# A three-block kernel: where the folded weights' loads stand in the first phase's written order

## The chip, the cores and the metric

The kernel runs on one core of a Trainium2 chip. The metric is the time of one execution on the device in microseconds, as the median of several runs. One execution was also recorded by the hardware profiler; every row below is from that one.

## What is computed

Three blocks follow one another, for 4 batches of 576 tokens. Cut to what matters here:

```python
# 1: attention over a window of 128 keys, 8 heads of 64 -> x: 4 x 576 x 512
# 2: gated block
h = np.maximum(x @ w_in, 0.0)                     # 512 -> 1024
u, v = h[..., :512], h[..., 512:]
v_n = (v - mean(v)) / np.sqrt(var(v) + 1e-06)      # per token
v_s = einsum('ts,bsd->btd', w_spatial, v_n) + b_spatial
x = (u * v_s) @ w_out
# 3: four experts of attention (wq, wk, wv, wo), two of them chosen per token by x @ w_gate
```

Between block 2 and block 3 nothing stands but matrix products, so the kernel never forms the second block's output: it multiplies w_out by the third block's wq, wk, wv and w_gate once, and lets block 3 read G = u * v_s. That product is the fold, and its operands are the folded weights.

## The kernel before

**Two phases.** The first phase makes attention and the gated block for the four batches, one after another, and stores G in HBM. Then comes the fold (`fold`, line 937: 96 matmuls), and the second phase runs the experts.

**Split numbers.** Every float32 operand of a product is kept as two tiles, a rounded one (cast on ScalarE, `split`, line 265, or its like) and the remainder (a subtraction on VectorE, `lo_part`, line 261), and every product is three passes of matmuls over them (`PASSES`).

**The written order.** The first phase is a list of short names in three strings, OPENING, FIRST and SECOND. `step` (line 809) turns a name into instructions. Those that matter here, for batch b, tile of tokens t, half of the tokens s, and block of 128 columns m:

- `V.b.t.n`, `r`, `bn`, `ag`: v before its normalisation (12 matmuls of 128x512 in three passes), its eviction with the ReLU on ScalarE (line 723), its mean and variance on VectorE (lines 726 and 727).
- `n.b.t.ln`, `.ex`, `.r0` to `.r3`: one over the root of the variance, for tiles 0 to 2 at once (`normal_ops`, line 730; ScalarE lines 736 and 737, VectorE lines 738 to 741).
- `N.b.t.sc`, `.hi`, `.lo`: v scaled (VectorE line 745), rounded (ScalarE line 749), its remainder (VectorE line 263).
- `U.b.s.m.n`, `ur`: u (12 matmuls of 128x288, line 777) and its eviction with the ReLU (ScalarE line 780).
- `P.b.m.s.n`, `pm`, `gs`: v_s (line 792), the product with u on VectorE (line 800), the store of G by SP (line 877).

All of these products go through three PSUM banks (`psD`, line 247), so a product can only begin once the product three before it has been evicted.

**Who sets the order.** TensorE runs its matmuls as they are written, in the whole kernel. For ScalarE, VectorE, GpSimd and SP, a scheduler that simulates the program may reorder instructions, except where `written` holds (from line 242 to its closing): there they too run as written. OPENING stands within `written`; its last part is the end of batch 2 and the beginning of batch 3. FIRST and SECOND are the rest of batch 3, put in a queue (`Dense`) and pulled from between other steps.

**The folded weights' loads.** Behind OPENING, still within `written`, the program makes the loads of chunks 0 and 1 of wcat (wq, wk, wv and w_gate side by side, 128 rows of 772 each; `take_wcat`, line 900). Then `written` closes, and there follow the loads of chunks 2 and 3 and of w_out (`wt`, line 957), the four chunks' casts and remainders (`load_wcat`, line 932: lines 266 and 263), and the loads of batch 0's G (`load_g`, line 966: line 974), whose tail is cast into `both` (line 986). The program pulls FIRST in between:

```python
    for name in OPENING.split():
        step(name)
    ...
    for k in range(2):
        take_wcat(k)
    written.close()
    for name, names in (("u3_1", FIRST), ("s3", SECOND)):
        dense.add(rest(names), cost(names), name=name)
    ...
    for k in (2, 3):
        dense.pull(1000.0)
        later.popleft()()
    dense.through("u3_1")
```

All of these transfers are issued by SP, in one queue.

Of the kernel before, what the change touches and what calls it, by code (L numbers as in the profile page):

```python
# [103 lines left out]
    P2.0.0.2 pm2.3.1 gs2.3 a17 pm2.0.0 R18.1 pm2.0.1 gs2.0 xc17 P2.1.0.0 V3.3.0 xs17 xh17 R18.0 P2.2.0.0 P2.2.0.1 xl17 P2.1.0.1 P2.1.0.2 g18.1.0  # L104
    V3.3.1 g18.1.1 pm2.1.0 V3.3.2 g18.0.0 V3.1.0 r3.3 g18.0.1 bn3.3 V3.1.1 ag3.3 n3.3.ln V3.1.2 n3.3.ex n3.3.r0 n3.3.r1 P2.2.0.2 n3.3.r2 r3.1 n3.3.r3
    N3.3.sc a18 pm2.2.0 bn3.1 ag3.1 xc18 P2.2.1.0 P2.1.1.0 xs18 P2.2.1.1 xh18 P2.2.1.2 xl18 U3.1.0.0 pm2.2.1 P2.1.1.1 gs2.2 V3.2.0 N3.3.hi U3.1.0.1
    U3.1.0.2 V3.2.1 ur3.1.0 P2.1.1.2 V3.2.2
"""
FIRST = """
    pm2.1.1 N3.3.lo gs2.1 U3.1.3.0 r3.2 U3.1.3.1 bn3.2 U3.1.3.2 U3.1.2.0 ag3.2 n3.2.ln ur3.1.3 U3.0.2.0 n3.2.ex n3.2.r0 U3.1.2.1 n3.2.r1 n3.2.r2  # L110
    U3.1.2.2 n3.2.r3 N3.1.sc U3.0.2.1 N3.2.sc ur3.1.2 N3.1.hi U3.0.2.2 N3.0.sc N3.2.hi U3.0.3.0 N3.1.lo N3.0.hi U3.0.1.0 N3.2.lo ur3.0.2 U3.0.3.1
    N3.0.lo U3.0.3.2 P3.2.0.0 ur3.0.3 U3.0.1.1 P3.2.0.1 U3.0.1.2 P3.2.1.0 ur3.0.1 P3.2.0.2 P3.2.1.1 pm3.2.0 P3.1.0.0 P3.1.0.1 U3.1.1.0 P3.2.1.2
    P3.1.0.2 pm3.2.1 gs3.2 U3.1.1.1 pm3.1.0 U3.1.1.2 U3.0.0.0 ur3.1.1 P3.1.1.0 P3.0.0.0 U3.0.0.1 P3.0.0.1 U3.0.0.2
"""
SECOND = """
    P3.1.1.1 ur3.0.0 P3.1.1.2 P3.0.0.2 pm3.1.1 gs3.1 P3.0.1.0 pm3.0.0 P3.0.1.1 P3.0.1.2 P3.3.1.0 pm3.0.1 P3.3.1.1 gs3.0 P3.3.0.0 P3.3.0.1 P3.3.1.2
# [1255 lines left out]
```

## Time and profile before

| | us |
|---|---|
| median of 3 runs | 432.82 |
| the runs | 433.19, 429.93, 432.82 |
| the profiled execution | 429.61 |
| its span, first to last instruction | 427.9 |
| TensorE busy (matmuls) | 410.8 (96% of the span) |
| VectorE, ScalarE, GpSimd busy | 316.0, 242.7, 171.2 |

The span is the part of the execution that the rows cover; 1.7 us lie around it. Busy time is the time in which an engine works on an instruction, not that in which it waits for one. TensorE's granted clock is 1.00, its higher level (2.4 GHz), in all forty slices of the span.

### The profile page before, as it was taken

The page shows a single profiled execution, that of the slowest core. Times are in us where ns is not written, and L with a number is a line of the kernel's source. Part 1 is how long each engine was busy: PE and PEld are TensorE (multiplying, and loading weights), DVE is VectorE, ACT ScalarE, POOL GpSimd, SP SyncE. Part 2 cuts the span into 40 slices and gives each one's busy share as a digit, 9 for nine tenths or more (in the row PEclk, how much of TensorE's full clock was granted, in tenths as well). Part 3 has the DMA queues.
Part 4 walks back from the last instruction along what each step waited for, and adds up shares of the span by engine and source line. Part 5 has one row for each costly group of instructions (what it writes and reads, how often), then busy time and mean ns, then how long its engine had stood idle before and what let it go on. Part 6 is the DMA issues. An engine that isn't in the chain of part 4 may idle for free.

```text
span 427.9 us, 12099 instructions
## 1 busy us (share of the span) xinstructions
PE 410.8 (96%) x4399; PEld 367.5 (86%) x4399; DVE 316.0 (74%) x1061; ACT 242.7 (57%) x757; POOL 171.2 (40%) x265
## 2 busy tenths in 40 slices
PE   6789999999999999999996999999999999999996
PEld 5567798799899998899996999999999998988884
DVE  5998999999899968796445322649888788678541
ACT  6898768847465465463225202656666557556642
POOL 3575644537306644432300000139665653544100
PEclk9999999999999999999999999999999999999999
DMA  8997367858846865324294170211879978898884
GB/s 258 383 289 284 111 180 209 277 138 273 263 145 156 266 182 159 95 76 108 60 347 158 42 230 2 58 54 26 214 203 279 250 158 242 210 269 223 221 261 126
DMA packets 76943, 80.06 MB, mean 187 GB/s; under 512 B 18002, under 2 KB 52946, under 8 KB 76500
## 3 DMA queue, kind: packets, MB, share of 16 engines
q1 hardware_dynamic: 76740, 79.15, 63.2%
q8 instruction: 35, 0.57, 0.6%
q14 instruction: 24, 0.20, 0.1%
q10 hardware_dynamic: 144, 0.13, 0.1%
HBM read 49.64 MB, written 29.62 MB: 185 GB/s over the span
## 4 chain that ended last, share of the span: by engine, by line
PE 73%; DMA 8%; ACT 7%; DVE 6%; POOL 2%; issue 2%; SPq 2%; DVEq 0%; ACTq 0%; POOLq 0%
PE pq L1042 12%; PE pg L792 10%; PE pv L714 7%; PE pu L777 7%; PE pvB L1070 6%; PE pxB L1239 6%; PE pout_None L1257 6%; PE psB L1136 4%; PE pw L946 4%; ACT p L286 3%; DMA st_wc<-in_wcat 3%; DMA raw<-in_w_in 3%; DMA carry<-p 3%; PE px L679 3%; PE pg L795 2%
## 5 line engine op out<-in xcount | busy, mean ns | idle before, releaser
L286 ACT ACTIVATE p<-p,st 128x128 f32<-128x128 f32 x144 | 56.5, 396 | 23.3 <-DVE st L285 13.4
L792 PE MATMUL pg<-wsp,vn 128*128 128x288 f32 x384 | 59.9, 297 | 2.1 <-ACT vn L749 2.0
L777 PE MATMUL pu<-x,win 128*128 128x288 f32 x384 | 58.6, 298 | 2.0 <-ACT u L780 1.7
L777 PEld LDWEIGHTS pu<-x,win 128*128 128x128 f32 x384 | 53.5, 188 | 5.1 <-ACT u L780 2.2
L792 PEld LDWEIGHTS pg<-wsp,vn 128*128 128x128 f32 x384 | 54.1, 188 | 4.4 <-ACT vn L749 2.2
L714 PE MATMUL pv<-win,x 128*128 128x512 f32 x216 | 57.3, 398 | 0.3 <-ACT x L700 0.3
L565 POOL TENSOR_TENSOR p<-p,st 128x512 f32<-128x512 f32 (+1 forms) x28 | 32.4, 1161 | 61.5 <-DVE st L563 29.2
L1042 PE MATMUL pq<-x,W 128*128 128x288 f32 x384 | 56.8, 297 | 0.0
L1042 PEld LDWEIGHTS pq<-x,W 128*128 128x128 f32 x384 | 52.5, 188 | 1.6 <-issue 0.8
L1160 ACT ACTIVATE pB<-pB,stB 128x128 f32<-128x128 f32 (+4 forms) x72 | 41.7, 581 | 13.7 <-DVE stB L1152 7.5
L298 POOL TENSOR_SCALAR pB<-pB,stB 128x384 f32<-128x384 f32 (+4 forms) x64 | 35.9, 581 | 28.8 <-DVE stB L1169 13.8
L714 PEld LDWEIGHTS pv<-win,x 128*128 128x128 f32 x216 | 38.4, 188 | 8.3 <-issue 1.0
L1152 DVE CUSTOM_DVE_ANT_0 pB<-psB,trit 128x128 f32<-128x128 f32 (+3 forms) x64 | 27.9, 485 | 6.0 <-PE psB L1136 5.7
L285 DVE CUSTOM_DVE_ANT_0 p<-ps,relm 128x128 f32<-128x128 f32 x128 | 30.1, 281 | 3.0 <-DMA carry<-p 2.8
L1186 DVE STREAM_TRANSPOSE pB<-pB 128x1024 f32<-128x1024 f32 (+3 forms) x28 | 26.9, 980 | 1.7 <-POOL pB L298 1.7
L286 ACT ACTIVATION_READ_ACCUMULATOR p<-p,st 128x1 f32 x144 | 27.5, 191 | 0.0
L602 POOL TENSOR_SCALAR_AFFINE_SELECT pU<-pT 128x512 f32<-128x512 f32 (+1 forms) x26 | 18.7, 727 | 21.1 <-DMA pT<-carry 21.0
L1070 PE MATMUL pvB<-W,x 128*128 128x260 f32 x192 | 27.1, 284 | 0.0
L1239 PE MATMUL pxB<-pTB,vt 128*64 128x128 f32 (+2 forms) x480 | 26.4, 260 | 0.0
L1257 PE MATMUL pout_None<-wo,o 128*128 128x512 f32 x102 | 26.3, 401 | 0.0
L1239 PEld LDWEIGHTS pxB<-pTB,vt 128*64 128x64 f32 (+1 forms) x480 | 23.2, 136 | 2.8 <-issue 1.1
L1070 PEld LDWEIGHTS pvB<-W,x 128*128 128x128 f32 x192 | 24.7, 188 | 0.8 <-issue 0.7
(195 smaller groups left out, 932.9 us busy)
## 6 DMA issues: line engine op xcount, KB each, us to landing
carry<-p SPq DMA_DIRECT2D x96, 64.0 KB, 2.4
pT<-carry SPq DMA_DIRECT2D x24, 256.0 KB, 3.1
q<-in_qP SPq DMA_DIRECT2D x20, 256.0 KB, 3.5
g_dram<-g SPq DMA_DIRECT2D x16, 288.0 KB, 3.6
gf<-g_dram SPq DMA_DIRECT2D x16, 288.0 KB, 5.0
raw<-in_w_in SPq DMA_DIRECT2D x8, 512.0 KB, 6.6
v<-in_v SPq DMA_DIRECT2D x16, 256.0 KB, 4.3
mid<-pB SPq DMA_DIRECT2D x16, 256.0 KB, 4.9
```

The costliest lines, as they stand in the source:

```text
L285: lambda: nc.vector.tensor_tensor_reduce(s_view, ps_view, tab, -0.125, FLT_MAX, ALU.add, ALU.min, nm),
L286: lambda: nc.scalar.activation(s_view, s_view, AF.Exp, bias=nm, scale=-1.0, accum_out=sm),
L298: nc.gpsimd.tensor_scalar(p, p, r, 0.0, op0=ALU.mult, op1=ALU.add)
L565: ops["m"] = lambda: nc.gpsimd.tensor_tensor(blocks, blocks, sm.unsqueeze(1).unsqueeze(3).to_broadcast([P, 4, n, 32]), op=ALU.mult)
L714: nc.tensor.matmul(pv, x[i][:, k, t0 : t0 + P], win[j][:, k, 512:1024], start=(n == 0 and k == 0), stop=(n == 2 and k == 3))
L777: nc.tensor.matmul(pu[:, :HALF], win[i][:, k, m * P : (m + 1) * P], x[j][:, k, c], start=(n == 0 and k == 0), stop=(n == 2 and k == 3))
L792: nc.tensor.matmul(pg[:, :HALF], vn[i][k][:, m * P : (m + 1) * P], wsp[j][:, k, c], start=(n == 0 and k == 0), stop=False)
L1042: nc.tensor.matmul(pq[:, :HALF], W[i][c0 // CUT][:, k, c0 % CUT : c0 % CUT + P], G[j][:, k, c], start=(n == k == 0), stop=(n == 2 and k == 3))
L1070: nc.tensor.matmul(pv[:, :260], rows, W[j][1][:, k, 512 - CUT :], start=(n == k == 0), stop=(n == 2 and k == 3))
L1160: nc.scalar.activation(part(i), part(i), AF.Exp, bias=st[:, i : i + 1], scale=-1.0, accum_out=st[:, 4 + i : 5 + i])
L1239: nc.tensor.matmul(px[64 * o : 64 * o + 64, pr, :qn], vt[:kb, c, (2 * pr + o) * 64 : (2 * pr + o) * 64 + 64], rhs(pr, c, o), start=(c == 0 ...
L1257: nc.tensor.matmul(po[:, : c.stop - c.start], o2[i][:, pr, :], wos[j][:, pr, c], start=(n == pr == 0), stop=(n == 2 and pr == 1))
```

## The change

36 names go from FIRST to the end of OPENING, in the same sequence: from the last product of batch 2 (`pm2.1.1`) through v's normalisation of batch 3 and its last remainder (`N3.0.lo`). The rest of the program's text stays as it is. So for these steps the four engines beside TensorE run in the order of the names, and the two loads that stand behind OPENING (chunks 0 and 1 of wcat) come after them.

```diff
@@ OPENING, its end
-    U3.1.0.2 V3.2.1 ur3.1.0 P2.1.1.2 V3.2.2
+    U3.1.0.2 V3.2.1 ur3.1.0 P2.1.1.2 V3.2.2 pm2.1.1 N3.3.lo gs2.1 U3.1.3.0 r3.2 U3.1.3.1 bn3.2 U3.1.3.2 U3.1.2.0 ag3.2 n3.2.ln ur3.1.3 U3.0.2.0
...
+    N3.0.hi U3.0.1.0 N3.2.lo ur3.0.2 U3.0.3.1 N3.0.lo
@@ FIRST, its beginning
-    pm2.1.1 N3.3.lo gs2.1 U3.1.3.0 r3.2 U3.1.3.1 bn3.2 U3.1.3.2 U3.1.2.0 ag3.2 n3.2.ln ur3.1.3 U3.0.2.0 n3.2.ex n3.2.r0 U3.1.2.1 n3.2.r1 n3.2.r2
...
+    U3.0.3.2 P3.2.0.0 ur3.0.3 U3.0.1.1 P3.2.0.1 U3.0.1.2 P3.2.1.0 ur3.0.1 P3.2.0.2 P3.2.1.1 pm3.2.0 P3.1.0.0 P3.1.0.1 U3.1.1.0 P3.2.1.2 P3.1.0.2
```

ScalarE, from the eviction of v's tile 2 of batch 3 on, before. A name ends in a number of the build; `wc00` and `wc01` are the rounded chunks 0 and 1, `vr3_2` is v of batch 3, tile 2, `vn0_1` its rounded tile 1, `u3` is u's column block 3, and `both0_0` is the tail of batch 0's G.

```order
L723 ACTIVATE vr3_2_3606<-pv3_2_3516 128x512
L266 CAST wc00_3578<-st_wc0_3545 128x772
L780 ACTIVATE u3_109<-pu3_3_1_3601 128x288
L736 ACTIVATE vs3_3176<-vs3_3176,eps_147 128x3
L266 CAST wc01_3579<-st_wc1_3547 128x772
L737 ACTIVATE vs3_3176<-vs3_3176 128x3
L780 ACTIVATE u2_108<-pu3_2_1_3619 128x288
L780 ACTIVATE u2_108<-pu3_2_0_3627 128x288
L749 CAST vn0_1_111<-vr3_1_3438 128x512
L749 CAST vn0_2_112<-vr3_2_3606 128x512
L780 ACTIVATE u3_109<-pu3_3_0_3661 128x288
L749 CAST vn0_0_110<-vr3_0_3224 128x512
```

The same place now, as far as the next eviction of u:

```order
L736 ACTIVATE vs3_3176<-vs3_3176,eps_147 128x3
L780 ACTIVATE u3_109<-pu3_3_1_3548 128x288
L737 ACTIVATE vs3_3176<-vs3_3176 128x3
L780 ACTIVATE u2_108<-pu3_2_1_3564 128x288
L749 CAST vn0_1_111<-vr3_1_3438 128x512
L749 CAST vn0_2_112<-vr3_2_3553 128x512
L749 CAST vn0_0_110<-vr3_0_3224 128x512
L780 ACTIVATE u2_108<-pu3_2_0_3572 128x288
L986 CAST both0_0_3799<-gf0_3786 128x4x64
L780 ACTIVATE u3_109<-pu3_3_0_3604 128x288
L266 CAST wc00_3656<-st_wc0_3623 128x772
L266 CAST wc01_3657<-st_wc1_3625 128x772
```

The two casts moved from ahead of v's normalisation to behind it; behind them now stands the eviction of u's block 1. The cast of G's tail stood behind v's last rounding and ahead of that eviction, and now stands ahead of the second eviction of block 3. On VectorE the two remainders moved in the same way, from ahead of line 738 to ahead of the first product of batch 3 (line 800).

SP, from the first store of G in this stretch on, before (`g2_2` is G of batch 2, block 2; `gf0` is batch 0's G on its way back):

```order
L877 DMA g_dram_84<-g2_2_3476 128x576
L902 DMA st_wc0_3545<-in_wcat 128x772
L902 DMA st_wc1_3547<-in_wcat 128x772
L957 DMA wt1_3577<-wt_dram_83 128x512 x2
L974 DMA gf0_3786<-g_dram_84 128x576 x4
L877 DMA g_dram_84<-g2_1_3401 128x576
```

And now:

```order
L877 DMA g_dram_84<-g2_2_3476 128x576
L957 DMA wt1_3655<-wt_dram_83 128x512 x2
L974 DMA gf0_3786<-g_dram_84 128x576 x4
L877 DMA g_dram_84<-g2_1_3401 128x576
L902 DMA st_wc0_3623<-in_wcat 128x772
L902 DMA st_wc1_3625<-in_wcat 128x772
```

The two loads moved behind the last two pieces of w_out, the four loads of G and one store.

## Rows read from the trace of the kernel before

**Rows 1.** Waits of TensorE, whole run: us in total, times, longest.

```profile
PE pg L792 <- ACT vn L749: 2.0, 1, 2.0
PE pu L777 <- ACT u L780: 1.7, 2, 1.2
```

**Rows 2.** Busy time by stage: PE, PEld, DVE, ACT, POOL, clock, DMA, GB/s.

```profile
220.00:225.00 5.00, 4.64 (x35) 4.41 (x34) 0.88 (x2) 0.83 (x2) 0.00 (x0) 1.00 1.03 398
224.00:232.00 8.00, 4.25 (x28) 3.56 (x28) 5.76 (x12) 5.02 (x12) 0.64 (x1) 1.00 0.64 243
232.00:253.00 21.00, 20.93 (x153) 20.70 (x152) 6.22 (x12) 3.60 (x8) 0.43 (x3) 1.00 0.34 113
253.00:300.00 47.00, 47.00 (x344) 45.35 (x343) 25.25 (x75) 22.12 (x61) 15.08 (x26) 1.00 0.15 43
```

**Rows 3.** Timeline of TensorE: start us, us, what, idle before and its releaser.

```profile
219.70 4.94 PE L777 MATMUL pu<-x,win 128*128 128x288 f32 x36
225.87 0.80 PE L777 MATMUL pu<-x,win 128*128 128x288 f32 x4 [1.22 <-ACT u L780]
227.18 1.84 PE L777 MATMUL pu<-x,win 128*128 128x288 f32 x12 [0.52 <-ACT u L780]
231.03 0.80 PE L792 MATMUL pg<-wsp,vn 128*128 128x288 f32 x4 [2.00 <-ACT vn L749]
...
233.24 1.22 PE L792 MATMUL pg<-wsp,vn 128*128 128x288 f32 x8
...
234.56 1.75 PE L792 MATMUL pg<-wsp,vn 128*128 128x288 f32 x12
236.15 0.70 PE L777 MATMUL pu<-x,win 128*128 128x288 f32 x4
...
250.57 2.61 PE L946 MATMUL pw<-wc,wt 128*128 128x384 f32 x14
```

**Rows 4.** Timeline of ScalarE.

```profile
219.90 0.60 ACT L723 ACTIVATE vr<-pv 128x512 f32<-128x512 f32 x1 [1.34 <-PE pv L714]
224.67 0.83 ACT L266 CAST wc<-st_wc 128x772 fp32r<-128x772 f32 x1 [4.17 <-DMA st_wc<-in_wcat]
225.41 0.40 ACT L780 ACTIVATE u<-pu 128x288 f32<-128x288 f32 x1
225.71 0.29 ACT L736 ACTIVATE vs<-vs,eps 128x3 f32<-128x3 f32 x1
...
229.02 1.14 ACT L749 CAST vn<-vr 128x512 fp32r<-128x512 f32 x2 [1.59 <-DVE vr L745]
```

**Rows 5.** Timeline of VectorE: tile 3's statistics and scaling, then tile 2's.

```profile
207.96 0.18 DVE L727 BATCH_NORM_AGGREGATE vs<-vs 128x2 f32<-128x6 f32 x1
...
209.51 0.55 DVE L745 TENSOR_SCALAR vr<-vr,vs 128x512 f32<-128x512 f32 x1
...
221.26 0.18 DVE L727 BATCH_NORM_AGGREGATE vs<-vs 128x2 f32<-128x6 f32 x1
225.54 0.96 DVE L263 TENSOR_TENSOR wc<-st_wc,wc 128x772 fp32r<-128x772 f32 x1 [4.09 <-ACT wc L266]
...
228.44 1.46 DVE L745 TENSOR_SCALAR vr<-vr,vs 128x512 f32<-128x512 f32 x3
```

**Rows 6.** Timeline of SP's issues: start us, us, what.

```profile
217.13 1.40 SPq L902 DMA_DIRECT2D st_wc<-in_wcat  x2
...
220.47 2.64 SPq L974 DMA_DIRECT2D gf<-g_dram  x4
224.71 20.46 SPq L877 DMA_DIRECT2D g_dram<-g  x3
```

**Rows 7.** DMA, 215:231 (busy in 40 slices; issues, KB, us to landing), then 217.1:217.5.

```profile
DMA  9999887999999999999999999999999999410000
...
gf<-g_dram SPq DMA_DIRECT2D x4, 288.0 KB, 7.1
...
st_wc<-in_wcat SPq DMA_DIRECT2D x1, 386.0 KB, 7.5
```

More of the change, by code (lines that the diff above doesn't have):

```diff
@@ L106 @@
     N3.3.sc a18 pm2.2.0 bn3.1 ag3.1 xc18 P2.2.1.0 P2.1.1.0 xs18 P2.2.1.1 xh18 P2.2.1.2 xl18 U3.1.0.0 pm2.2.1 P2.1.1.1 gs2.2 V3.2.0 N3.3.hi U3.1.0.1
-    U3.1.0.2 V3.2.1 ur3.1.0 P2.1.1.2 V3.2.2
+    U3.1.0.2 V3.2.1 ur3.1.0 P2.1.1.2 V3.2.2 pm2.1.1 N3.3.lo gs2.1 U3.1.3.0 r3.2 U3.1.3.1 bn3.2 U3.1.3.2 U3.1.2.0 ag3.2 n3.2.ln ur3.1.3 U3.0.2.0
+    n3.2.ex n3.2.r0 U3.1.2.1 n3.2.r1 n3.2.r2 U3.1.2.2 n3.2.r3 N3.1.sc U3.0.2.1 N3.2.sc ur3.1.2 N3.1.hi U3.0.2.2 N3.0.sc N3.2.hi U3.0.3.0 N3.1.lo
+    N3.0.hi U3.0.1.0 N3.2.lo ur3.0.2 U3.0.3.1 N3.0.lo
 """
 FIRST = """
-    pm2.1.1 N3.3.lo gs2.1 U3.1.3.0 r3.2 U3.1.3.1 bn3.2 U3.1.3.2 U3.1.2.0 ag3.2 n3.2.ln ur3.1.3 U3.0.2.0 n3.2.ex n3.2.r0 U3.1.2.1 n3.2.r1 n3.2.r2
-    U3.1.2.2 n3.2.r3 N3.1.sc U3.0.2.1 N3.2.sc ur3.1.2 N3.1.hi U3.0.2.2 N3.0.sc N3.2.hi U3.0.3.0 N3.1.lo N3.0.hi U3.0.1.0 N3.2.lo ur3.0.2 U3.0.3.1
-    N3.0.lo U3.0.3.2 P3.2.0.0 ur3.0.3 U3.0.1.1 P3.2.0.1 U3.0.1.2 P3.2.1.0 ur3.0.1 P3.2.0.2 P3.2.1.1 pm3.2.0 P3.1.0.0 P3.1.0.1 U3.1.1.0 P3.2.1.2
-    P3.1.0.2 pm3.2.1 gs3.2 U3.1.1.1 pm3.1.0 U3.1.1.2 U3.0.0.0 ur3.1.1 P3.1.1.0 P3.0.0.0 U3.0.0.1 P3.0.0.1 U3.0.0.2
+    U3.0.3.2 P3.2.0.0 ur3.0.3 U3.0.1.1 P3.2.0.1 U3.0.1.2 P3.2.1.0 ur3.0.1 P3.2.0.2 P3.2.1.1 pm3.2.0 P3.1.0.0 P3.1.0.1 U3.1.1.0 P3.2.1.2 P3.1.0.2
+    pm3.2.1 gs3.2 U3.1.1.1 pm3.1.0 U3.1.1.2 U3.0.0.0 ur3.1.1 P3.1.1.0 P3.0.0.0 U3.0.0.1 P3.0.0.1 U3.0.0.2
 """
```

## The prediction

> **What bounds the kernel now.** I read the waits of TensorE first. In the whole run it waits little, and the two largest entries behind the first 40 us are neighbours: 2.0 us for the rounded tiles of v, once, and 1.7 us for u's evictions, twice [rows 1]. The busy time by stage says where. TensorE has 4.64 us of work in the 5 us from 220 to 225 and 4.25 in the 8 us from 224 to 232, and from 232 on it is full: 20.93 of 21 us, then 47.00 of 47 [rows 2]. So TensorE is the bound, and one hole, 224 to 232, belongs to the stretch that the change rewrites.
>
> Its size comes from the starts of the matmuls. A 128x288 matmul takes 0.1325 us when nothing is in its way: twelve lie between the starts at 234.56 and 236.15 [rows 3]. The 36 that begin at 219.70 would let the next start at 224.47; it starts at 225.87, 1.40 late. Four more (0.53) end at 226.40; the next start is at 227.18, 0.78 late. Twelve more (1.59) end at 228.77; the first gating matmul of batch 3 (pg3_2_0) starts at 231.03, 2.26 late. Together 4.43 us [rows 3], somewhat over the 3.7 us that the waits sum to, because a restart also refills the pipeline.
>
> Who makes the hole stands in the rows of ScalarE and VectorE. ScalarE takes v's last tile out at 219.90 and next has the cast of the folded weights' chunk 0, which starts at 224.67 after 4.17 us of waiting for its load [rows 4]. Behind it in the same queue stand the eviction of u that TensorE needs first (225.41), the logarithm of the normalisation, the second cast, and so on to the rounding of v's tiles from 229.02 [rows 4]. VectorE is in the same place: the statistics of tile 2 are aggregated at 221.26, and its next instruction is chunk 0's remainder at 225.54, 4.09 us of waiting for that cast; the three scalings follow at 228.44 [rows 5]. The load itself was issued at 217.13 and took 7.5 us, in a burst in which the loads of batch 0's G take 7.1 [rows 6, 7]; the engines that move data are full from 215 to about 229 us [rows 7], at 398 GB/s [rows 2].
>
> **The change part by part.** Nothing is computed more or less; TensorE's own order is the same instruction for instruction, and GpSimd's too. Two loads (386 KB each), two casts and two remainders move.
>
> Removed from the path: on ScalarE and VectorE the wait for chunk 0 and the four instructions between v's statistics and its normalisation. What is late next? The chain from aggregate to scaling stands undisturbed in the same trace for tile 3: 207.96 to 209.51, 1.55 us [rows 5]. From 221.26 that gives 222.81; one eviction of u stands between logarithm and exponential now, at most 0.3 us more, as its neighbours in ScalarE's queue start 0.30 apart (225.41 to 225.71) [rows 4]: 223.1. Three scalings take 1.46 [rows 5], so 224.6. The two casts of v at 229.02 take 1.14 together [rows 4]; three take 1.7, and they begin behind u's eviction that waits for TensorE's 28th matmul of the 36 (219.70 + 3.71 = 223.4, evicted near 224.0): last cast near 225.6. TensorE, running through, comes to pg3_2_0 at 219.70 + 52 x 0.1325 = 226.6. So v is ready 1 us before it is asked for, and each of the three starts that were late is covered: the whole 4.43 us is open to be won.
>
> Put in elsewhere, three things. First, the two loads are issued behind w_out's last pieces, G of batch 0 and one store of G. They cost issue time on SP only, but the landing matters. The load of chunk 0 now has the place in SP's queue that the last load of G had, which was issued about 222.8 (220.47 + 2.64, less its own issue) [rows 6]. The bytes of the burst are the same, and it ends about 229 us by the share of busy transfer engines [rows 7]; that last load of G took 7.1, landing at 229.9 [rows 6, 7]. I take the end of the burst, 229.0 to 229.9, as landing of the last folded load (chunk 1), middle 229.5.
>
> Second, on ScalarE the casts now stand ahead of the eviction of u's column block 1 (u1_107 out of pu3_1_0), and on VectorE the remainders stand ahead of the first gating product (g3_2). Counted from pg3_2_0, TensorE wants the bank of the former 4.06 us later (in before, 231.03 to 234.56 plus four matmuls) and that of the latter 5.12 us later (236.15) [rows 3], now 230.7 and 231.7. Cast of chunk 1 at 229.5 for 0.83 [rows 4], eviction of 0.4 behind it: free near 230.6. Remainder from 230.4 for 0.96, product of 0.45 behind it: near 231.7. Both arrive with nothing to spare: 0 to 0.5 us of new waiting; I take 0.2.
>
> Third, the cast of G's tail (both0_0) is now ahead of the eviction of u's block 3 (pu3_3_0), whose bank TensorE wants 2.21 us after pg3_2_0 (233.24) [rows 3], now 228.8. G's loads have two loads fewer ahead: 2 x 395 kB at 398 GB/s [rows 2] is 2.0 us, so the last lands near 227.9, the tail is cast by 228.3, the eviction is done near 228.6. Hidden, by 0.2 us; if that cover goes, it is the same sub-microsecond wait.
>
> The Trainium skill (DMA: Bandwidth & Descriptors, section "Where 436 GB/s comes from") says that for transfers between HBM and SBUF HBM's share of a core binds, about 358 GB/s; this trace shows 398 in that stretch [rows 2], so the lower rate does not bind here. By that page's rate the last 6.5 us before 229.5 would stretch to an estimated 7.2, and the sum would lose another 0.7 us.
>
> Sum: -4.43 + 0.2 = -4.2 us. Where does it go afterwards? Behind 232 us TensorE has no wait in the list [rows 1, 2], and the loads of batch 1's G wait for casts that wait for TensorE, so all of it moves forward together. The profiled execution takes 429.61 (span 427.9 and 1.7 around it) and would take 425.4. The runs shown are 429.93, 432.82 and 433.19, so the profiled one lies 3.2 under their median of 432.82, by nothing this trace explains. On the median the forecast is 432.82 - 4.2 = 428.6 us.
>
> Bounds. Upper end of the gain: 4.43, no new wait. Lower end of this case: chunk 1's load takes the 7.5 us that the folded load at 217.13 took [rows 7], from an issue at 222.8, and lands at 230.3; that is 0.7 of waiting, and with a restart of up to 0.3 the gain is 3.4. On the median 428.4 to 429.4.
>
> **The rivals.**
> Partly given back: a new wait takes the place of the old. Beyond 229.6 us each microsecond by which chunk 1 lands late is one of waiting. If SP issues the two loads only where it now issues the store ahead of them, 224.71 [rows 6], they land 7.5 us on, about 232.2; the new wait is 2.6 and the gain 1.8: 431.0 us. For it: SP stood 1.6 us before that store. Against: it stood there for the landing of chunk 0's load, which is no longer ahead of it.
>
> Given back downstream: the gain is real at 232 us but phase two is paced by transfers. 432.8 us, no change. Against: TensorE full from 253 to 300 with hardly any traffic, 43 GB/s [rows 2].
>
> Slower: both casts now block ScalarE's queue in front of evictions that TensorE needs, where before they blocked it one stage earlier. It decides from a landing of chunk 1 at 229.6 + 4.4 = 234.0. With two latencies of 7.5 us [rows 7] in a row, each load waiting for the one before, it would be 222.8 + 15 = 237.8: 3.8 us slower, 436.6. Against: two loads were in flight together in before, issued back to back at 217.13 [rows 6].
>
> That the change does not do what it says is half true: of four chunks only 0 and 1 move, chunks 2 and 3 stay ahead as before. TensorE has no wait for them: the two entries above are the largest behind the first 40 us, and both belong to the hole [rows 1, 3]. So that costs nothing.
>
> **How the numbers follow.** A measurement of this kernel tells about 1% (4.3 us) from no change. Main case 0.64; partly given back 0.19; no change 0.10; slower 0.07. The main case lies right at the 1% line, 4.2 against 4.33. The runs of before lie in two groups 3 us apart with the median in the upper, so a median in the lower group would read as clearly faster; I count 0.45 of the main case as faster, 0.19 as same. With 0.01 of the partial case: faster 0.46, same 0.47, slower 0.07. The range goes from the lower group's full gain, 425.2, down to 425.0, to the partial case and a little more, 431.5.
>
> **What would show it.** Right: no wait of TensorE over 0.5 us between 220 and 235; logarithm near 221.5; pg3_2_0 near 226.6; casts of chunks 0 and 1 near 228.5 and 229.5; first fold matmul near 246.4 in place of 250.57 [rows 3]. Wrong in the middle step: ScalarE's largest wait there is again for the folded load, now behind 229.6, with evictions of u or products of G late after it. Wrong at the end: fold 4 us earlier, span not.

## The result, and the profile after

| | before | after |
|---|---|---|
| median, 7 runs each, us | 432.82 | 427.33 |
| lowest and highest | 429.55 to 434.32 | 425.77 to 428.70 |
| the profiled execution | 429.61 | 428.70 |
| its span | 427.9 | 426.8 |

The ratio of after to before is 0.9891, with a 95% interval of 0.9852 to 0.993: faster by 1.1%.

The two profiled executions are only 0.9 us apart, so the gain can't be read from their spans. After's execution came to the stretch in question late: the 36 matmuls of u that [rows 3] begin with start at 222.13 in place of 219.70, in the main because of waits far ahead of the change. So everything below is counted from that start, called the anchor here. The waits of TensorE after, the largest ahead of the anchor and behind 60 us, and the only one from 215 to 255:

```profile
PE px L679 <- POOL pT L602: 1.6, 2, 1.4
...
PE pg L792 <- ACT u L780: 0.9, 1, 0.9
```

The first is attention's and has nothing to do with the names that moved; over the ten executions profiled in all the anchor lies between 219.70 and 222.43, and the same program differs by as much as 2.1 us in it. The second is in the place of the two entries of [rows 1]. The busy time by stage answers to the first three rows of [rows 2], each window set 2.43 us later, as the anchor is:

```profile
222.43:227.43 5.00, 5.00 (x39) 5.00 (x39) 3.46 (x11) 2.57 (x8) 0.00 (x0) 1.00 1.05 399
226.43:234.43 8.00, 7.12 (x53) 6.76 (x53) 3.89 (x7) 4.59 (x10) 0.74 (x1) 1.00 0.59 231
234.43:255.43 21.00, 20.93 (x147) 20.70 (x147) 7.62 (x15) 4.07 (x8) 0.13 (x2) 1.00 0.41 138
```

TensorE is busy in all of the first 5 us, in 7.12 of the 8 us in which it had 4.25 before, and in 20.93 of the 21 us behind them, as before. The transfers run at the same rate in the first window, 399 GB/s against 398. The starts of its matmuls, against [rows 3]:

```profile
222.13 7.05 PE L777 MATMUL pu<-x,win 128*128 128x288 f32 x52
...
229.01 0.69 PE L792 MATMUL pg<-wsp,vn 128*128 128x288 f32 x4
...
231.17 1.32 PE L792 MATMUL pg<-wsp,vn 128*128 128x288 f32 x8
...
232.60 0.69 PE L792 MATMUL pg<-wsp,vn 128*128 128x288 f32 x4
234.17 1.33 PE L792 MATMUL pg<-wsp,vn 128*128 128x288 f32 x8 [0.88 <-ACT u L780]
...
249.74 2.44 PE L946 MATMUL pw<-wc,wt 128*128 128x384 f32 x13
```

The 36, 4 and 12 matmuls of u that stood in three rows are one row of 52, and the first gating matmul (pg3_2_0) starts 6.88 us behind the anchor; before it was 11.33. Later, at 234.17, stands the new wait. The fold starts 27.61 behind the anchor; before, 30.87.

ScalarE, VectorE and SP, against [rows 4 to 6]:

```profile
222.32 0.60 ACT L723 ACTIVATE vr<-pv 128x512 f32<-128x512 f32 x1 [1.49 <-PE pv L714]
...
223.91 0.30 ACT L736 ACTIVATE vs<-vs,eps 128x3 f32<-128x3 f32 x1 [0.98 <-DVE vs L727]
...
226.36 1.65 ACT L749 CAST vn<-vr 128x512 fp32r<-128x512 f32 x3
...
230.40 0.41 ACT L986 CAST both<-gf 128x256 fp32r<-128x256 f32 x1 [2.08 <-DMA gf<-g_dram]
...
232.03 1.78 ACT L266 CAST wc<-st_wc 128x772 fp32r<-128x772 f32 x2 [0.91 <-DMA st_wc<-in_wcat]
233.72 0.40 ACT L780 ACTIVATE u<-pu 128x288 f32<-128x288 f32 x1
```

```profile
223.69 0.18 DVE L727 BATCH_NORM_AGGREGATE vs<-vs 128x2 f32<-128x6 f32 x1
...
225.44 1.46 DVE L745 TENSOR_SCALAR vr<-vr,vs 128x512 f32<-128x512 f32 x3
...
232.90 1.90 DVE L263 TENSOR_TENSOR wc<-st_wc,wc 128x772 fp32r<-128x772 f32 x2 [4.00 <-ACT wc L266]
```

```profile
225.16 1.99 SPq L902 DMA_DIRECT2D st_wc<-in_wcat  x2
```

Behind v's last eviction ScalarE now goes straight to the logarithm, 1.78 after the anchor, and v's three casts stand together. The casts of both chunks run back to back from 232.03, 9.90 behind the anchor, after a wait for a load. The eviction of u's block 1 stands right behind them at 233.72, and TensorE, which would have taken its bank at 233.13 (232.60 and four matmuls of 0.1325), gets it at 234.17. By these rows nothing but the order of ScalarE's queue holds that eviction, and the experiment with GpSimd below bears it out: the last matmuls of that u stand ahead of the product that starts at 231.17.

Everything behind goes through unchanged. The last piece of the chain that ends last:

```profile
422.91 0.37 ACT ot L1265
```

It starts 173.17 us behind the first fold matmul (422.91 - 249.74), before as after, and between 173.16 and 173.18 in all ten profiles. So what a version gains behind the anchor is how much nearer its fold comes to it, 3.26 us in this pair.

### The profile page after: what moved, and what is told of

The parts are those of the page before. It is cut to its first block, busy times and chain, and to the rows that moved or that the text cites. A ratio compares the mean times of both kernels' runs of the same rounds, so it can differ in the third digit from the quotient of the medians.

```text
span 426.8 us, 12095 instructions
## 1 busy us (share of the span) xinstructions
PE 411.0 (96%) x4399; PEld 367.6 (86%) x4399; DVE 316.6 (74%) x1061; ACT 243.1 (57%) x757; POOL 171.2 (40%) x265
## 4 chain that ended last, share of the span: by engine, by line
PE 77%; DMA 10%; DVE 4%; SPq 3%; ACT 3%; issue 1%; POOL 1%; DVEq 0%; POOLq 0%; ACTq 0%
PE pq L1042 12%; PE pu L777 10%; PE pg L792 9%; PE pv L714 9%; PE pvB L1070 6%; PE pxB L1239 6%; PE pout_None L1257 6%; PE psB L1136 4%; PE pw L946 4%; PE px L679 2%; DMA v<-in_v 2%; DMA carry<-p 2%; PE px L650 2%; DMA reltail<-in_relt 2%; DMA st_wc<-in_wcat 1%; DMA raw<-in_w_in 1%
## 5 line engine op out<-in xcount | busy, mean ns | idle before, releaser
L298 POOL TENSOR_SCALAR pB<-pB,stB 128x384 f32<-128x384 f32 (+4 forms) x64 | 35.9, 580 | 28.8 <-DVE stB L1169 14.3
L1257 PE MATMUL pout_None<-wo,o 128*128 128x512 f32 x102 | 26.3, 401 | 0.0
```

The lines of the kernel that those rows point to most:

```text
L298: nc.gpsimd.tensor_scalar(p, p, r, 0.0, op0=ALU.mult, op1=ALU.add)
L1257: nc.tensor.matmul(po[:, : c.stop - c.start], o2[i][:, pr, :], wos[j][:, pr, c], start=(n == pr == 0), stop=(n == 2 and pr == 1))
```

## The experiments

One table for all of them, from the profiled executions, in us. "v ready" is from the anchor to the first gating matmul of batch 3, "fold" from the anchor to the first fold matmul. Removing the 4.43 of [rows 3] and putting in nothing would bring the fold to 30.87 - 4.43 = 26.44.

| kernel | v ready | fold | profiled execution | ratio to before [95%] |
|---|---|---|---|---|
| before | 11.33 | 30.87 | 429.61 | |
| before, profiled a second time | 11.47 | 31.03 | 430.06 | |
| before, profiled a third time | 11.05 | 32.14 | 432.90 | |
| after | 6.88 | 27.61 | 428.70 | 0.9891 [0.9852, 0.993] |
| order alone | 10.96 | 32.31 | 431.52 | 1.000 [0.9979, 1.002] |
| three names | 6.89 | 27.56 | 426.70 | 0.9922 [0.9898, 0.9946] |
| before, casts on GpSimd | 6.89 | 26.55 | 427.12 | 0.9907 [0.9886, 0.9927] |
| after, casts on GpSimd | 6.89 | 26.33 | 425.82 | 0.9879 [0.9858, 0.9899] |
| loads still further behind | 6.88 | 26.81 | 426.65 | 0.9903 [0.988, 0.9927] |
| a third load ahead | 6.89 | 28.09 | 429.20 | one execution |

**Which part does it: the written order alone.** All 36 names written out as in after, but the two loads issued from the place in the sequence where they stood before:

```diff
-    for name in OPENING.split():
+    for n, name in enumerate(OPENING.split()):
+        if n == 1330:
+            for k in range(2):
+                take_wcat(k)
         step(name)
-    for k in range(2):
-        take_wcat(k)
```

> The changed kernel with the two loads of chunks 0 and 1 put back to their old place (before the 36 moved names); the 36 names stay in the written order. Two distances are read, both from the start of u's 36 matmuls on TensorE: to the first gating matmul of batch 3 (11.33 us in before, 6.88 in after) and to the first fold matmul (30.87 and 27.61). Theory (the place of the loads decides, because ScalarE and VectorE wait in order for a load that has not landed): the wait is back, 11.3 and 30.9, time as before (ratio near 1.00). Rival (the written order of the normalisation decides): 6.9 and 27.6, ratio near 0.99.

The median is 431.11 against 431.03 of before on the same chip. The hole is back; TensorE's timeline and then the cast of chunk 0 on ScalarE:

```profile
220.47 4.94 PE L777 MATMUL pu<-x,win 128*128 128x288 f32 x36
...
226.75 0.79 PE L777 MATMUL pu<-x,win 128*128 128x288 f32 x4 [1.35 <-ACT u L780]
...
227.89 2.65 PE L777 MATMUL pu<-x,win 128*128 128x288 f32 x12 [0.34 <-ACT u L780]
...
231.43 1.33 PE L792 MATMUL pg<-wsp,vn 128*128 128x288 f32 x4 [0.90 <-ACT u L780]
...
252.78 3.49 PE L947 MATMUL pw<-wc,wt 128*128 128x384 f32 x19
```

```profile
225.37 0.83 ACT L266 CAST wc<-st_wc 128x772 fp32r<-128x772 f32 x1 [4.11 <-DMA st_wc<-in_wcat]
```

The 4.11 us of waiting for the load answer to the 4.17 of [rows 4]. That the normalisation is written out is worth nothing by itself; the place of the loads is what decides. (This execution also lost TensorE's clock for a while; see below.)

**How little of the change is needed.** Before, with three names moved and not 36, so that the loads stand behind one more store of G:

```diff
-    U3.1.0.2 V3.2.1 ur3.1.0 P2.1.1.2 V3.2.2
+    U3.1.0.2 V3.2.1 ur3.1.0 P2.1.1.2 V3.2.2 pm2.1.1 N3.3.lo gs2.1
```

> Before with only the first three of the 36 names moved (the last product of batch 2, a remainder of v, the store of G), so that the two loads stand behind that store, and v's normalisation is left to the scheduler. Theory (the place of the loads decides): as after, 6.9 us to the first gating matmul and 27.6 to the fold, ratio near 0.99. Rival (the written order of the normalisation decides): 11.3 and 30.9, ratio 1.00.

Median 427.26. Counted from the anchor it is as in after, with the same new wait:

```profile
220.28 7.05 PE L778 MATMUL pu<-x,win 128*128 128x288 f32 x52
...
227.17 0.69 PE L793 MATMUL pg<-wsp,vn 128*128 128x288 f32 x4
...
232.26 1.32 PE L793 MATMUL pg<-wsp,vn 128*128 128x288 f32 x8 [0.88 <-ACT u L781]
```

So the other 33 names add nothing: it is enough that the loads stand behind that store.

**Queue or transfer: the two chunks on GpSimd.** SP's loads stay where they were; the casts and remainders of chunks 0 and 1 go from ScalarE and VectorE to GpSimd, once in before and once in after:

```diff
+        if k < 2:
+            nc.gpsimd.tensor_scalar(wc[0][k], raw_[k], 1.0, 0.0, op0=ALU.mult, op1=ALU.add)
+            lo_part(wc[1][k], raw_[k], wc[0][k], nc.gpsimd)
```

> Before with nothing moved, but the cast and the remainder of chunks 0 and 1 made on GpSimd, which has 0.6 us of work between 224 and 232 us. The loads are issued where they were. Theory (the hole is made by ScalarE's and VectorE's queues waiting in order): the hole goes with no new wait, 6.9 us to the first gating matmul and 26.4 to 26.6 to the fold, 1 us better than after, ratio near 0.988. Rival (the hole is made by the transfers, the place of the loads in the burst): 11.3 and 30.9, ratio 1.00. A third way: GpSimd is so slow that chunk 1 is not ready when the fold asks for it; then the wait stands before the fold.

> After with the cast and the remainder of chunks 0 and 1 on GpSimd. It tells what the new wait of 0.88 us in after hangs on (TensorE at 234.17 on an eviction of u). Theory (the casts ahead of that eviction): the wait goes, 6.9 us to the first gating matmul and 26.4 to 26.6 to the fold, ratio near 0.987. Rival (the tail of G, cast ahead of an eviction since the change, or the bank itself): it stays, fold at 27.6, ratio near 0.989.

In before, with loads and written order untouched, the hole is gone and the new wait doesn't come (median 427.12). TensorE, then GpSimd:

```profile
221.48 7.05 PE L777 MATMUL pu<-x,win 128*128 128x288 f32 x52
228.37 0.69 PE L792 MATMUL pg<-wsp,vn 128*128 128x288 f32 x4
...
248.03 8.23 PE L954 MATMUL pw<-wc,wt 128*128 128x384 f32 x46
```

```profile
226.40 1.35 POOL L939 TENSOR_SCALAR wc<-st_wc 128x772 fp32r<-128x772 f32 x1 [11.72 <-DMA st_wc<-in_wcat]
227.83 2.17 POOL L263 TENSOR_TENSOR wc<-st_wc,wc 128x772 fp32r<-128x772 f32 x1
...
```

GpSimd stands idle for 11.72 us until the load lands, and that costs nothing: what waits with it has no reader near. That settles that it was the order of ScalarE's and VectorE's queues, and not the transfers as such. In after the same edit takes away the new wait:

```profile
220.60 7.05 PE L777 MATMUL pu<-x,win 128*128 128x288 f32 x52
...
246.93 9.29 PE L954 MATMUL pw<-wc,wt 128*128 128x384 f32 x52
```

The fold is at 26.33, 1.28 nearer than in after. This version has the nearest fold and the lowest median, 425.82 against 431.03 of before on the same chip: 0.9879, with an interval of 0.9858 to 0.9899. That interval overlaps those of all the other versions that gain, so its rank among them rests on the fold. Its fold is 0.11 nearer than the 26.44 that nothing put in would leave. That sum leaves out that the four matmuls behind the hole take 0.80 in [rows 3], and 0.69 in the row at 228.37 above.

**Where the loads should stand.** Before, with 54 names moved, through the store `gs3.2`, so that the loads are issued 11.3 us later than in after, 14.34 behind the anchor (235.45) in place of 3.03:

```diff
-    U3.1.0.2 V3.2.1 ur3.1.0 P2.1.1.2 V3.2.2
+    U3.1.0.2 V3.2.1 ur3.1.0 P2.1.1.2 V3.2.2 pm2.1.1 N3.3.lo gs2.1 U3.1.3.0 r3.2
...
+    P3.2.0.0 ur3.0.3 U3.0.1.1 P3.2.0.1 U3.0.1.2 P3.2.1.0 ur3.0.1 P3.2.0.2 P3.2.1.1 pm3.2.0 P3.1.0.0 P3.1.0.1 U3.1.1.0 P3.2.1.2 P3.1.0.2 pm3.2.1 gs3.2
```

> Before with 54 names moved in place of 36, so that the two loads stand behind the first store of batch 3's G and are issued some 8 us later than in after; ScalarE's casts of chunks 0 and 1 then stand behind both evictions of u's block 1, VectorE's remainders behind the first three products. Theory (a late load costs nothing unless its cast stands ahead of an eviction that TensorE is about to need): no wait, 6.9 us to the first gating matmul, 26.3 to 26.6 to the fold, ratio near 0.988. Rival (a folded load has only to be early; 8 us later it is late for the fold): a wait before the first fold matmul or at the casts of G in front of it, 27.6 or more to the fold, ratio 0.99 or above.

Median 426.79. TensorE, then ScalarE:

```profile
221.11 7.05 PE L777 MATMUL pu<-x,win 128*128 128x288 f32 x52
...
242.23 1.87 PE L792 MATMUL pg<-wsp,vn 128*128 128x288 f32 x12 [0.56 <-DVE g L800]
...
```

```profile
238.64 0.84 ACT L266 CAST wc<-st_wc 128x772 fp32r<-128x772 f32 x1 [1.81 <-DMA st_wc<-in_wcat]
239.38 1.82 ACT L976 CAST x<-gf 128x576 fp32r<-128x576 f32 x3
241.10 0.83 ACT L266 CAST wc<-st_wc 128x772 fp32r<-128x772 f32 x1
```

The wait of after at u's block 1 is gone, and a smaller one, which was not expected, has come 9 us later (21.12 behind the anchor, after: 12.04), for a product of G that on VectorE now stands behind chunk 0's remainder and two remainders of batch 0's G. The fold is 0.80 nearer than in after, at 26.81 and not within the 26.3 to 26.6 expected. Later is better than after's place, but moving a blocking instruction along an in-order queue only picks whom it blocks. Its ratio lies within the intervals of after and of the three names, so the order among these three is told by the profiles alone.

**What sets the new wait: a third load ahead.** After, with one more load of a chunk's size that nothing reads, issued in front of G's loads:

```diff
+    spare = [fp.tile([P, NW], F32, name=f"spare{i}") for i in range(1)]
+    for t in spare:
+        nc.sync.dma_start(t, wcat[256:384, :])
```

> After with one more load of 386 KB into a tile that nothing reads, issued behind w_out's last piece and so ahead of G of batch 0 and of the two moved loads; the scheduler puts the eviction of u's block 1 between the two casts. Theory (in after the transfers' rate sets the new wait, one microsecond of lateness is one of waiting): 395 kB at 400 GB/s are 1.0 us, so the tail of G and the casts come 1.0 us later and the fold 0.7 to 1.2 us later than in after, 28.3 to 28.8 us from the start of u's matmuls; 6.9 to the first gating matmul stays. Rival (the wait is the length of the casts and remainders themselves): 27.6 as in after, or less, as the eviction stands one cast earlier.

It ran once, so its positions are read and not its time. TensorE, then ScalarE:

```profile
222.43 7.05 PE L777 MATMUL pu<-x,win 128*128 128x288 f32 x52
...
232.94 1.33 PE L792 MATMUL pg<-wsp,vn 128*128 128x288 f32 x8 [1.35 <-ACT u L780]
...
```

```profile
232.17 0.40 ACT L989 CAST both<-gf 128x256 fp32r<-128x256 f32 x1 [3.54 <-DMA gf<-g_dram]
...
233.76 0.84 ACT L266 CAST wc<-st_wc 128x772 fp32r<-128x772 f32 x1 [0.88 <-DMA st_wc<-in_wcat]
```

G's tail is cast 9.74 behind the anchor (after: 8.27) and the first chunk 11.33 (after: 9.90): 386 KB more ahead moved both by 1.4 to 1.5 us, more than the 1.0 that 395 kB take at the 398 GB/s of [rows 2]. The fold lost only 0.48. The wait went to another place, for the eviction behind G's tail, and the one behind the chunks vanished, with u's block 1 put between them by the scheduler. So the fold, at 28.09, fits neither the theory's 28.3 to 28.8 nor the rival's 27.6. That one more load ahead brings the landings later is shown. That its bytes alone do it is not, since SP also issued the first of the two loads 2.07 us later behind the anchor (227.53, 5.10; after: 3.03). How a late landing becomes a wait depends on who stands behind it.

**Before, twice more.** The kernel before, unchanged, in two more executions, for how the hole varies.

> Before, unchanged, a second look. In the profile of the kernel with the loads put back, TensorE's granted clock fell behind the hole and the fold came 1.4 us later than in before's own profile. Theory (the hole costs its 4.4 us always, and in some executions a fall of the clock on top): here 11.3 us to the first gating matmul, and to the fold either 30.9 with the clock at 1.00 or 32 to 33 with the clock under 1.00 between 226 and 238 us. Rival (the fall belongs to the reordered kernel alone): 30.9 and clock 1.00 in both looks.

> Before, unchanged, a third look, for the same question as the second. From the first fold matmul to the end of the chain 173.17 us were measured in each of the six profiles so far; that is expected here too, so that an execution's time is the start of u's 36 matmuls plus the distance to the fold plus 173.2 and about 6 us around it.

The first repeated the profile ahead of the prediction. In the second of the two the fold is 32.14 behind the anchor and not 30.9 to 31.0. Busy time by stage there, columns as in [rows 2], and the same matmuls in TensorE's timeline:

```profile
232.00:236.00 4.00, 3.19 (x17) 3.19 (x17) 1.49 (x3) 1.06 (x3) 0.93 (x1) 0.73 0.01 2
236.00:240.00 4.00, 4.00 (x27) 4.00 (x27) 0.45 (x1) 0.41 (x1) 0.00 (x0) 0.85 0.00 0
...
```

```profile
232.81 0.80 PE L792 MATMUL pg<-wsp,vn 128*128 128x288 f32 x4 [1.99 <-ACT vn L749]
...
234.08 1.16 PE L792 MATMUL pg<-wsp,vn 128*128 128x288 f32 x4
...
```

Four matmuls that take 0.69 at the higher level took 1.16. The order-alone kernel shows the same: granted clock 0.71 and then 0.62 in the stretches around its waits (0.50, which is the lower level of 1.2 GHz, in 230 to 235 us), before it is 1.00 again:

```profile
226.70:231.40 4.70, 3.44 (x16) 2.86 (x16) 4.51 (x11) 3.12 (x9) 0.00 (x0) 0.71 0.61 229
231.40:236.70 5.30, 5.27 (x26) 5.27 (x27) 0.69 (x2) 0.98 (x3) 0.73 (x1) 0.62 0.01 2
236.70:250.00 13.30, 13.23 (x100) 13.00 (x99) 5.31 (x10) 3.11 (x6) 0.00 (x0) 1.00 0.16 53
```

So the hole has a second price, 1.1 to 1.4 us (32.14 - 31.03 and 32.31 - 30.87), in two of the four executions profiled with it. In these two the hole itself was 0.3 to 0.5 us shorter. From the first gating matmul to the fold alone, the table gives 19.54 and 19.56 us with the clock at 1.00, and 21.09 and 21.35 here: 1.5 to 1.8 us more.

## Why the prediction was right, and where it was off

The forecast of 428.6 us stands against 427.33, inside the range of 425.0 to 431.5, and after is the faster kernel, by an interval that leaves out no change.

**The cause of the hole, and that it goes whole: right, and shown.** 4.43 was forecast, 4.45 went (11.33 to 6.88). The logarithm was forecast at 1.8 behind the anchor and came at 1.78, pg3_2_0 at 6.9 and came at 6.88. That the in-order queues make it, and not a shortage of data, the GpSimd version of before shows.

**G's tail: right.** Forecast at 8.2 behind the anchor (227.9), cast at 8.27; the matmuls behind it start 0.05 late: at 231.17 in place of 231.12, which is 2.11 behind pg3_2_0's 229.01, as in after with the casts on GpSimd. The next product is 0.15 late (232.33; 3.32 behind pg3_2_0 and not 3.17). So the eviction behind the tail was not quite hidden.

**The new wait: right in its place and mechanism, off in size.** "0 to 0.5 us of new waiting; I take 0.2" measured 1.17 (27.61 - 26.44). The step that failed is the time at which the last folded load lands. "Middle 229.5" for chunk 1 was 9.8 behind the anchor, and chunk 0's cast was put at 228.5, 8.8 behind. The casts came at 9.90 and at about 10.8, each a microsecond late, and by the prediction's own rule, "Beyond 229.6 us each microsecond by which chunk 1 lands late is one of waiting", that is the wait. So the sign that it named, "no wait of TensorE over 0.5 us between 220 and 235", did not come true (0.88), and the fold, forecast at 246.4 or 26.7 behind the anchor, came at 27.61.

Where the microsecond comes from stands in the issues. In before, the last transfer of the burst is the store of G that SP issues at 224.71 [rows 6]; in after that store stands ahead of the two loads, and the last is chunk 1. The store of before, with its KB and the us to its landing; then chunk 1 of after, its issue and its landing:

```profile
g_dram<-g SPq DMA_DIRECT2D x1, 288.0 KB, 5.9
```

```profile
226.81 0.33 SPq L902 DMA_DIRECT2D st_wc<-in_wcat  x1
```

```profile
st_wc<-in_wcat SPq DMA_DIRECT2D x1, 386.0 KB, 6.1
```

Before's last landing is at 230.6, 10.9 behind the anchor, and after's at 232.9, 10.8 behind. So the premise that the burst ends where it did held. What was wrong is the reading of that end: the prediction took it from the share of busy transfer engines (229.0) and from the landing of the last load of G (229.9), and left out the store that landed 0.7 later. SP issued the first load where forecast (225.16 is 3.03 behind the anchor, forecast 3.1), and the rate was the forecast's, 399 GB/s against the 398 of [rows 2]. The Trainium skill (DMA: Bandwidth & Descriptors, section "Where 436 GB/s comes from") gives about 358 GB/s for transfers between HBM and SBUF; both rows lie above it, so the 0.7 us that the prediction worked out by that page's rate is not where the wait comes from. The lower bound of the case, landing after another 7.5 us with 0.7 of waiting and 0.3 of restart, was the better row; yet the 3.26 us of this pair lie just under the 3.4 that it gave.

**All of it passes through: right.** 173.17 us from fold to the chain's last piece before and after, so nothing is given back downstream, and 3.26 us (3.42 against before's second profile) is the gain where TensorE's clock stays up.

**Onto the median: a hit that is partly luck.** The medians differ by 5.5 in the first comparison, and 3.8 and 4.1 separate before from the three names and from the later loads in the others. The interval of the ratio stands for 3.0 to 6.4 us, so the times can't tell the 4.2 forecast from the 3.26 of the profiles; the 4.2 is a microsecond too high, as the new wait was put at 0.2. The prediction saw two groups in before's three runs, 3 us apart "by nothing this trace explains"; the seventeen runs of before in the second comparison fill 428.56 to 432.92 with no gap of 1 us. Part of that spread can be the clock, which costs 1.1 to 1.4 us where it falls, and which the forecast didn't count: with the hole it fell in two of four executions, and in the six profiled without it the granted clock is 1.00 in 215 to 230 and in 230 to 255. So few don't show that its fall went with the hole. Another part is the anchor, which moves by over 2 us from one execution to the next; the clock is not what moves it, since it is 1.00 all the way there in after and in the third profile of before, whose anchors are late (222.13 and 221.76).

## What to carry to other kernels

An instruction that waits for a load blocks everything written behind it on its engine: look at what stands behind it, and ask of each who is waiting for that. Put it on an engine whose queue has no urgent reader (here GpSimd, at a slower rate and with the nearest fold). Moved along the same queue it only chooses another victim. A load that lands before the turn of its cast would block nothing, but no version here reaches that: even in the latest one ScalarE waits 1.81 us for chunk 0. When you forecast the end of a burst of transfers, take the landing of the last one in the queue, stores too. And compare two profiles from a common event just ahead of the change, not by their spans, when executions differ by as much as the gain.

## What the runs showed of the hardware that was not expected

TensorE's granted clock fell in the stretch of three short waits, none of which was longer than 2.0 us: to the lower of its two levels (0.50, 1.2 GHz) in 230 to 235 us of the order-alone kernel, and to 0.62 to 0.85 on average over the stretches shown; four matmuls of 128x288 took 1.16 us in place of 0.69. Much the same waits in two other executions of before left the clock at 1.00. What tells the two apart, these runs don't show. It also fell far ahead of the anchor, to 0.83 in 20 to 30 us, in four of the ten executions, three of them without the hole.

GpSimd's two casts of 128x772 took 0.84 us each in the GpSimd version of after, and 1.35 and 1.27 in that of before; the remainders took 1.85 and 1.84, and 2.17 and 1.84. ScalarE takes 0.83 for the cast and VectorE 0.96 for the remainder [rows 4, 5]. The first pair in after's version:

```profile
230.34 0.84 POOL L939 TENSOR_SCALAR wc<-st_wc 128x772 fp32r<-128x772 f32 x1 [0.42 <-DMA st_wc<-in_wcat]
231.25 1.85 POOL L263 TENSOR_TENSOR wc<-st_wc,wc 128x772 fp32r<-128x772 f32 x1
...
```
